# A second xT buffer, one q/k buffer, w2 ahead of batch 2's loads, and attention paced per batch, in a fused attention and feed-forward kernel

## The chip, the cores and the metric

The kernel runs on one core of a Trainium2 chip. The metric is device time in microseconds (us), the median of several executions. A program on one core has no second die to compare with, so a run counts as slow only when it is over 1.5% above the fastest of its kernel. TensorE is the matmul engine (PE in the profile), VectorE is DVE, ScalarE is ACT, GpSimd is POOL, and SyncE is SP.

## The reference

Relu-squared attention over 8 batches, 12 heads, 448 tokens and 64 columns a head, followed by a feed-forward block with layer norm and a residual:

```python
scores = (q @ k.transpose(0, 1, 3, 2)) / np.sqrt(64)
attn   = np.maximum(scores, 0.0) ** 2 / 448
x      = (attn @ v)                       # heads joined: (8, 448, 768)
xn     = (x - mu) / np.sqrt(var + 1e-06) * g_ln
out    = x + np.maximum(xn @ w_ch1, 0.0) @ w_ch2     # 768 -> 3072 -> 768
```

Batches are counted from 0 here, so "batch 2" is the third. Inputs and output are fp32, the kernel computes in bf16, and its loads cast while they move.

## The kernel before

The feed-forward work is done in four units of two batches. Attention of later batches is threaded between its matmuls: each piece of feed-forward work has a cost, and a target says how many attention steps must be out by then. So the order of the pieces matters: in the trace below TensorE stands for 3.57 us at one product with v while feed-forward matmuls come next in its program. Names in the code and the profile: QK are the matmuls of the scores (sc), AV those with v, at the squared scores, xT the attention output x with its columns on the partitions, x_t the same x with tokens on the partitions, xc the centred x that goes into the feed-forward, h1 the output of the first feed-forward pass. These parts matter (the rest is cut):

```python
io_pool = ctx.enter_context(tc.tile_pool(name="qkv", bufs=2))   # q, k, v
xT_pool = ctx.enter_context(tc.tile_pool(name="xT", bufs=1))
...
def load_batch(b, pieces):            # all on GpSimd's queue, with the cast
    ...                               # from batch 2 on q and k head by head: 24 loads of 56 KB
def att_T(i, ...):                    # head pair i: q and k transposed
    if b >= PE_T:                     # from batch 2 on by DMA, on SyncE's queue
        for t, sb in enumerate((q_sb, k_sb)):
            nc.sync.dma_start_transpose(qkT_t[:, t, :]..., sb[:, 2*pr:2*pr+2, :]...)
def att_AV(i, ...):
    ...                               # 8 matmuls, then VectorE:
    nc.vector.tensor_scalar(xT_of(b, pr), ps, c2, None, op0=Alu.mult)
def ffn_x(u, ki):                     # tokens back to partitions, for statistics and residual
    nc.sync.dma_start_transpose(x_tok[u][:, :, ki*P:(ki+1)*P], xT[u][:, ki, :])
...
load_batch(2, ALL)                    # batch 2, then w2
for c in range(W2C):
    load_w2(c)
...
def pull():                           # emits an attention step; then
    while nload < B and ai >= steps_of(nload - 2):
        load_batch(nload, ALL)        # batch 3 as soon as batch 1's attention is emitted
```

xT holds the attention output of the two batches of a unit. `ffn_x` reads it, and attention of the next unit overwrites it.

Of the kernel before, what the change touches and what calls it, by code (L numbers as in the profile page):

```python
# [11 lines left out]
def kernel(  # L12
# [10 lines left out]
    nc = tc.nc  # L23
    P = 128
    bf16 = mybir.dt.bfloat16
# [4 lines left out]
    B, H, S, D = q.shape  # L30
# [5 lines left out]
    NJ = 4  # L36
    SP = S // NJ
    NPAIR = H // 2
    K1 = d_model // P
    K2 = d_ff // P  # L40
    U = 2
# [6 lines left out]

    const_pool = ctx.enter_context(tc.tile_pool(name="const", bufs=1))
    w_pool = ctx.enter_context(tc.tile_pool(name="w_pool", bufs=1))  # L50
    io_pool = ctx.enter_context(tc.tile_pool(name="qkv", bufs=2))
    t_pool = ctx.enter_context(tc.tile_pool(name="qkT", bufs=3))
    attn_pool = ctx.enter_context(tc.tile_pool(name="attn", bufs=7))
    xT_pool = ctx.enter_context(tc.tile_pool(name="xT", bufs=1))
    xs_pool = ctx.enter_context(tc.tile_pool(name="xs", bufs=1))
    xc_pool = ctx.enter_context(tc.tile_pool(name="xc", bufs=2))
    x_pool = ctx.enter_context(tc.tile_pool(name="x", bufs=1))
# [16 lines left out]
    h1 = h_pool.tile([P, K2, UT], bf16)  # L74
# [2 lines left out]


    qkv = {}

    PE_T = 2

    def load_batch(b, pieces):

        if b not in qkv:
            q_sb = io_pool.tile([SP, H, NJ * D], bf16, tag="q_sb")
            k_sb = io_pool.tile([SP, H, NJ * D], bf16, tag="k_sb")
            v_sb = io_pool.tile([SP, H, NJ * D], bf16, tag="v_sb")
            qkv[b] = (q_sb, k_sb, v_sb)
        q_sb, k_sb, v_sb = qkv[b]  # L90
        pairs = {"q": (q_sb, q), "k": (k_sb, k), "v": (v_sb, v)}
        for name, h0, hs in pieces:
            sb, src = pairs[name]
            if b >= PE_T and name != "v":

                by_pair = sb.rearrange("p (a x) (j d) -> p a (x j d)", x=2, j=NJ)
                by_pair = by_pair.rearrange("p a (j x d) -> p a j x d", x=2, j=NJ)
                for a in range(h0 // 2, (h0 + hs) // 2):
                    for x in range(2):
                        nc.gpsimd.dma_start(  # L100
                            by_pair[:, a, :, x, :],
                            src[b, 2 * a + x].rearrange("(p j) d -> p j d", j=NJ))
                continue
            nc.gpsimd.dma_start(  # L104
                sb[:, h0:h0 + hs, :],
                src[b, h0:h0 + hs].rearrange("h (p j) d -> p h (j d)", j=NJ),
            )

    g_sb = const_pool.tile([P, K1], fp32)

# [2 lines left out]
    def load_early():  # L113
# [10 lines left out]
            cast(dst, st)  # L124
        with nc.allow_non_contiguous_dma(reason="768 gains, once"):
            nc.sync.dma_start(g_sb, moe_g_ln.rearrange("(ko kp) -> kp ko", kp=P))

    ALL = [(n, 0, H) for n in "qkv"]

    CH = 512  # L130
    NCH = d_ff // CH
# [2 lines left out]
    def load_w1(c):  # L134
        nc.gpsimd.dma_start(w1[:, :, c * CH:(c + 1) * CH], w1_view[:, :, c * CH:(c + 1) * CH])
# [4 lines left out]
    def load_w2(c):  # L140
        ks = K2 // W2C
        nc.gpsimd.dma_start(w2[:, c * ks:(c + 1) * ks, :], w2_view[:, c * ks:(c + 1) * ks, :])

    def prep_w1(c, eng, k0, k1):
        for ki in range(k0, k1):
            w = w1[:, ki, c * CH:(c + 1) * CH]
            eng.tensor_scalar(w, w, g_sb[:, ki:ki + 1], None, op0=Alu.mult)  # L147


    xT = {}  # L150
# [5 lines left out]
    def att_T(i, half=None, evac=True):  # L156
        b, pr = divmod(i, NPAIR)
        q_sb, k_sb, _ = qkv[b]
        if b >= PE_T:
            if half == 0:  # L160
                return
            qkT_t = t_pool.tile([P, 2, S], bf16, tag="qkT")
            qkT[i] = qkT_t
            for t, sb in enumerate((q_sb, k_sb)):
                nc.sync.dma_start_transpose(
                    qkT_t[:, t, :].rearrange("p (j s) -> p j s", j=NJ),
                    sb[:, 2 * pr:2 * pr + 2, :].rearrange("p x e -> p (x e)"))
            return
        if half != 1:
            tp_ps = ps_m.tile([P, 2, S], bf16, tag="m")  # L170
            tp[0] = tp_ps
        ps = tp[0]
        for t, sb in enumerate((q_sb, k_sb)):
            if half is not None and t != half:
                continue
            for j in range(NJ):
                for hh in range(2):
                    nc.tensor.transpose(
                        ps[hh * D:(hh + 1) * D, t, j * SP:(j + 1) * SP],
                        sb[:, 2 * pr + hh, j * D:(j + 1) * D],  # L180
                        identity[:SP, :SP])
        if half == 0 or not evac:
            return
        att_T_out(i)

    def att_T_out(i):
        qkT_t = t_pool.tile([P, 2, S], bf16, tag="qkT")
        qkT[i] = qkT_t
        nc.vector.tensor_copy(qkT[i], tp[0])
# [61 lines left out]
    def ffn_x(u, ki):  # L251
        if ki == 0:
            x_t = x_pool.tile([P, MU, d_model], bf16, tag="x")
            x_tok[u] = x_t
        nc.sync.dma_start_transpose(x_tok[u][:, :, ki * P:(ki + 1) * P], xT[u][:, ki, :])  # L255
# [62 lines left out]
    att = []  # L318
# [6 lines left out]
    def step_b(i):  # L325
        att_QK(i, 2)
        att_QK(i, 3)
        if i > 0:
            att_AV(i - 1)
        if i + 2 < PE_T * NPAIR:  # L330
            att_T(i + 2)
        if PE_T * NPAIR <= i + 3 < NP_ALL:
            att_T(i + 3)

    def step_fine(i):
        att_QK(i, 0)
# [45 lines left out]
    def steps_of(b):  # L382
        return done_at[b]

    NU = B // U
    segs = []
    CPN = K2 // NCH
    for u in range(NU):
        for bb in range(U):
            items = []  # L390
            for ni in range(K2):
                if bb == 0 and u == 0 and ni % CPN == 0 and ni // CPN + 1 < NCH:
                    c = ni // CPN + 1
                    items.append((0.0, lambda c=c: prep_w1(c, nc.vector, K1 // 2 if c < 3 else 0, K1)))
                if bb == 1 and ni == 0:
                    for ki in range(K1):
                        items.append((0.0, lambda u=u, ki=ki: ffn_x(u, ki)))
                if bb == 1 and ni >= K2 - MU:
                    items.append((0.0, lambda u=u, m=ni - (K2 - MU): ffn_stats(u, m)))
                items.append((1.12, lambda u=u, bb=bb, ni=ni: ffn_1(u, bb, ni)))  # L400
            segs.append((u * U + bb, items))
        items = []
        for m in range(MU):
            for j in range(2):
                for part in range(4):
                    items.append((0.96, lambda u=u, m=m, j=j, p=part: ffn_2(u, m, j, p, 4)))
                    if m + j + part == 0:
                        items.append((0.0, lambda u=u: ffn_stats(u, MU)))
        segs.append((u * U + U - 1, items))
# [2 lines left out]
    ENGINES = [E.PE, E.Pool, E.DVE, E.Activation, E.SP]  # L412

    ai = 0
    nload = 3

    def pull():
        nonlocal ai, nload
        att[ai]()
        ai += 1  # L420
        while nload < B and ai >= steps_of(nload - 2):
            load_batch(nload, ALL)
            nload += 1

    with tc.manual_schedule(engines=set(ENGINES)):
        load_batch(0, [("v", 0, 4), ("q", 4, 4), ("k", 4, 4), ("v", 4, 4),
                       ("q", 8, 4), ("k", 8, 4), ("v", 8, 4)])
        load_early()
        load_w1(0)
        load_batch(1, ALL[:2])  # L430
        load_w1(1)
        load_batch(1, ALL[2:])
        for c in range(2, NCH):
            load_w1(c)
        for c in range(3):
            prep_w1(c, nc.gpsimd, 0, K1 // 2 if c else K1)
        warm_up(20)
        att_T(0)
        warm_up(5)
        while ai < steps_of(0):  # L440
            pull()
        load_batch(2, ALL)
        for c in range(W2C):
            load_w2(c)

        bounds = {}
        total = 0.0
        cum = []
        for need, items in segs:
            total += sum(c for c, _ in items)  # L450
            cum.append(total)
        t1 = cum[0]
        t_end = cum[-1] - sum(c for c, _ in segs[-1][1]) - sum(c for c, _ in segs[-2][1])
        n0, n1, n2 = steps_of(0), steps_of(1), len(att)

        def target(t):
            if t <= t1:
                return n0 + (n1 - n0) * t / (t1 - 3.0)
            return n1 + (n2 - n1) * (t - t1) / (t_end - 9.0 - t1)

        t = 0.0
        for need, items in segs:
            while ai < steps_of(need):
                pull()
            for cost, fn in items:
                fn()
                t += cost
                while ai < len(att) and ai + 1 <= target(t):
                    pull()
        assert ai == len(att) and nload == B  # L470


# [28 lines left out]
```

## Time and profile before

| | before |
|---|---|
| median of 3 runs | 587.07 us (586.45 to 588.53) |
| profiled span | 586.3 us |
| TensorE busy | 569.4 us |

First the busy table of the page (busy us, share of the span, instructions):

```profile
PE 569.4 (97%) x3542; PEld 289.1 (49%) x3542; DVE 262.5 (45%) x505; ACT 266.7 (45%) x392; POOL 142.5 (24%) x188
```

TensorE is the bottleneck, and a busy TensorE may still be at half clock. So look for its gaps and for stretches of low clock. The table by stretches of the kernel before (TensorE's idle time is the length less PE busy; then the other engines, the mean granted clock, the DMA share and GB/s):

```profile
72.40:90.00 17.60, 17.44 (x99) 8.23 (x98) 9.39 (x17) 11.72 (x19) 2.11 (x3) 1.00 1.18 192
90.00:112.00 22.00, 22.00 (x129) 10.19 (x127) 1.25 (x2) 14.54 (x24) 8.55 (x13) 1.00 1.53 166
112.00:126.00 14.00, 10.43 (x48) 4.38 (x45) 11.11 (x26) 4.48 (x6) 11.04 (x16) 0.76 1.93 170
126.00:136.00 10.00, 7.82 (x41) 3.78 (x40) 7.40 (x17) 3.63 (x5) 10.00 (x16) 0.83 1.43 85
...
220.00:240.00 20.00, 19.27 (x109) 8.71 (x108) 7.58 (x14) 11.58 (x20) 0.94 (x1) 1.00 0.83 121
```

The loss lies between 112 and 136 us: 5.75 us idle, and a clock of 0.76 and 0.83. The waits of that stretch name the first cause (who waited for what: us in total, times, longest; three of the lines):

```profile
DVE xT_t L230 <- DMA x_t<-xT_t: 20.2, 1, 20.2
...
PE av_ps L223 <- DVE at L200: 3.6, 1, 3.6
...
PE sc L197 <- ACT at L199: 2.2, 2, 1.8
```

VectorE may not write batch 2's output into xT until `ffn_x` has read it. It stands 20.2 us, then has a backlog, and TensorE waits for its squares. TensorE's timeline there (start, us, instructions; idle time and releaser in brackets):

```profile
108.22 3.58 PE L278 MATMUL ps<-xc_t,w_109 128*128 128x448 bf16 x18
111.73 0.58 PE L197 MATMUL sc<-qkT_t 64*112 64x448 bf16 x4
115.89 2.19 PE L223 MATMUL av_ps<-at,v_sb 112*64 112x448 bf16 x8 [3.57 <-DVE at L200]
118.01 4.37 PE L278 MATMUL ps<-xc_t,w_109 128*128 128x448 bf16 x12
```

Eighteen feed-forward matmuls take 3.58 us at full clock. After the gap twelve take 4.37 us, about half speed. The trace's clock records give half clock for 6.83 us from 115.1 and 3.41 us from 132.2.

What kept the transposes so long? SyncE's and GpSimd's queues (three lines of the first, four of the second):

```profile
79.40 5.22 SPq L165 DMA_TRANSPOSE qkT_t<-k_sb  x1
84.67 23.55 SPq L255 DMA_TRANSPOSE x_t<-xT_t  x6
108.31 1.21 SPq L165 DMA_TRANSPOSE qkT_t<-q_sb  x1
```

### The profile page before, as it was taken

The page shows a single profiled execution, that of the slowest core. Times are in us where ns is not written, and L with a number is a line of the kernel's source. Part 1 is how long each engine was busy: PE and PEld are TensorE (multiplying, and loading weights), DVE is VectorE, ACT ScalarE, POOL GpSimd, SP SyncE. Part 2 cuts the span into 40 slices and gives each one's busy share as a digit, 9 for nine tenths or more (in the row PEclk, how much of TensorE's full clock was granted, in tenths as well). Part 3 has the DMA queues.
Part 4 walks back from the last instruction along what each step waited for, and adds up shares of the span by engine and source line. Part 5 has one row for each costly group of instructions (what it writes and reads, how often), then busy time and mean ns, then how long its engine had stood idle before and what let it go on. Part 6 is the DMA issues. An engine that isn't in the chain of part 4 may idle for free.

```text
span 586.3 us, 8930 instructions
## 1 busy us (share of the span) xinstructions
PE 569.4 (97%) x3542; PEld 289.1 (49%) x3542; DVE 262.5 (45%) x505; ACT 266.7 (45%) x392; POOL 142.5 (24%) x188
## 2 busy tenths in 40 slices
PE   8989999789999999999999999999999999999996
PEld 5444444345555444445555444445555545556663
DVE  5967850194454433275453434257454435201111
ACT  6937866533233575663323465764313364440000
POOL 7788611683004600083002800000000000000000
PEclk9989999988999999999999999999999999999999
DMA  9999999999536909298264915610223141000111
GB/s 179 202 205 123 138 190 183 149 141 87 86 85 95 126 17 123 51 86 84 59 118 60 152 29 72 101 33 17 70 50 79 30 87 32 0 2 28 55 54 55
DMA packets 153242, 51.79 MB, mean 88 GB/s; under 512 B 125808, under 2 KB 149616, under 8 KB 153200
## 3 DMA queue, kind: packets, MB, share of 16 engines
q0 software_dynamic: 90144, 25.50, 44.6%
q1 hardware_dynamic: 62576, 25.25, 22.6%
q8 instruction: 28, 0.46, 0.3%
q10 hardware_dynamic: 480, 0.46, 0.3%
q14 instruction: 14, 0.11, 0.1%
HBM read 51.91 MB, written 11.01 MB: 107 GB/s over the span
## 4 chain that ended last, share of the span: by engine, by line
PE 76%; DMA 12%; DVE 4%; SPq 4%; POOL 3%; issue 1%; ACT 0%; DVEq 0%; POOLq 0%
PE o_ps L294 37%; PE ps L278 28%; DMA w_109<-in_moe_w_ch_dram 7%; PE sc L197 6%; PE av_ps L223 5%; DMA w_110<-in_moe_w_ch_dram 4%; SPq L255 3%; DMA x_t<-xT_t 2%; POOL k_sb L100 1%; DVE xc_t L245 1%; DVE at L200 1%; DVE stats L272 1%; POOL v_sb L104 1%; DVE stats L271 1%; POOL q_sb L100 1%
## 5 line engine op out<-in xcount | busy, mean ns | idle before, releaser
L278 PE MATMUL ps<-xc_t,w_109 128*128 128x448 bf16 x1152 | 232.2, 356 | 2.5 <-DVE xc_t L245 2.5
L294 PE MATMUL o_ps<-w_110,h_111 128*128 128x384 bf16 x1344 | 226.9, 327 | 0.0
L199 ACT ACTIVATE at<-sc 112x896 bf16<-112x896 f32 x192 | 165.1, 916 | 135.8 <-PE sc L197 132.2
L200 DVE TENSOR_TENSOR at<-at 112x896 bf16<-112x896 bf16 x192 | 118.9, 629 | 172.1 <-ACT at L199 172.1
L294 PEld LDWEIGHTS <-h_111 128*128 128x128 bf16 x1344 | 129.0, 98 | 96.4 <-issue 14.4
L278 PEld LDWEIGHTS <-w_109 128*128 128x128 bf16 x1152 | 109.4, 98 | 117.8 <-issue 21.5
L280 ACT ACTIVATE h_111<-ps 128x448 bf16<-128x448 f32 x192 | 104.6, 545 | 112.9 <-PE ps L278 112.8
L100 POOL DMA_DIRECT2D q_sb<-in_q_dram x72 | 50.2, 704 | 116.2 <-DMA qkT_t<-q_sb 53.1
L297 DVE SCALAR_TENSOR_TENSOR o_t<-o_ps,rstd_t,x_t 128x384 f32<-128x384 f32 x56 | 34.5, 616 | 76.9 <-PE o_ps L294 76.9
L197 PE MATMUL sc<-qkT_t 64*112 64x448 bf16 x384 | 59.7, 376 | 3.0 <-ACT at L199 2.7
L223 PE MATMUL av_ps<-at,v_sb 112*64 112x448 bf16 x384 | 48.7, 366 | 4.3 <-DVE at L200 3.6
L100 POOL DMA_DIRECT2D k_sb<-in_k_dram x72 | 50.0, 701 | 3.8 <-DMA q_sb<-in_q_dram 2.7
L230 DVE TENSOR_SCALAR xT_t<-av_ps 128x448 bf16<-128x448 f32 x48 | 29.7, 618 | 24.0 <-DMA x_t<-xT_t 20.2
L197 PEld LDWEIGHTS <-qkT_t 64*112 64x112 bf16 x384 | 18.6, 125 | 39.3 <-issue 37.2
L245 DVE TENSOR_TENSOR xc_t<-xT_t,mean_ps 128x448 bf16<-128x448 bf16 x48 | 26.2, 616 | 12.6 <-PE mean_ps L241 12.6
L223 PEld LDWEIGHTS <-v_sb 112*64 112x64 bf16 x384 | 17.8, 109 | 28.4 <-issue 22.1
L104 POOL DMA_DIRECT2D v_sb<-in_v_dram x10 | 8.9, 890 | 89.0 <-PE av_ps L223 88.3
L147 POOL TENSOR_SCALAR w_109<-w_109,g_sb 128x512 bf16<-128x512 bf16 x12 | 20.0, 1682 | 1.8 <-DVE w_109 L147 1.7
L272 DVE BATCH_NORM_STATS2 stats<-x_t 128x6 f32<-128x384 bf16 x28 | 15.2, 543 | 0.0
L271 DVE BATCH_NORM_STATS2 stats<-x_t 128x6 f32<-128x384 bf16 x28 | 14.6, 522 | 0.0
L315 PE MATMUL w_ps<-w_110,ones 128*128 128x256 bf16 x70 | 12.0, 315 | 1.2 <-DVE w_110 L76 1.2
L267 DVE RECIPROCAL rstd_t<-rstd_t 128x7 f32<-128x7 f32 x4 | 0.8, 200 | 26.7 <-ACT rstd_t L266 26.7
(32 smaller groups left out, 84.9 us busy)
## 6 DMA issues: line engine op xcount, KB each, us to landing
v_sb<-in_v_dram POOLq DMA_DIRECT2D x7, 672.0 KB, 10.1
w_109<-in_moe_w_ch_dram POOLq DMA_DIRECT2D x6, 768.0 KB, 25.6
w_110<-in_moe_w_ch_dram POOLq DMA_DIRECT2D x4, 1152.0 KB, 25.6
q_sb<-in_q_dram POOLq DMA_DIRECT2D x72, 56.0 KB, 3.9
k_sb<-in_k_dram POOLq DMA_DIRECT2D x72, 56.0 KB, 4.0
out_dram<-o_t SPq DMA_DIRECT2D x8, 336.0 KB, 3.0
out_dram<-o_t SPq DMA_DIRECT2D x8, 288.0 KB, 2.7
out_dram<-o_t SPq DMA_DIRECT2D x8, 240.0 KB, 2.8
```

The costliest lines, as they stand in the source:

```text
L100: nc.gpsimd.dma_start(by_pair[:, a, :, x, :], src[b, 2 * a + x].rearrange("(p j) d -> p j d", j=NJ))
L197: nc.tensor.matmul(sc[:SP, hh, :S], qkT[i][r, 1, t * SP:(t + 1) * SP], qkT[i][r, 0, :], start=True, stop=True)
L199: nc.scalar.activation(at, sc[:SP, :, :S], Act.Relu)
L200: nc.vector.tensor_mul(at, at, at)
L223: nc.tensor.matmul(ps[hh * D:(hh + 1) * D, :], v_sb[:, 2 * pr + hh, t * D:(t + 1) * D], attn[i, t][:, hh, :], start=(t == 0), stop=(t == N ...
L230: nc.vector.tensor_scalar(xT_of(b, pr), ps, c2, None, op0=Alu.mult)
L245: nc.vector.tensor_sub(xc_t[:, ki, :], xT_of(b, ki), mean_ps)
L272: nc.vector.bn_stats(stats[:, 1], x_tok[u][:, m, hd:])
L278: nc.tensor.matmul(ps, w1[:, ki, ni * P:(ni + 1) * P], xc[u * U + bb][:, ki, :], start=(ki == 0), stop=(ki == K1 - 1))
L280: nc.scalar.activation(h1[:, ni, bb * S:(bb + 1) * S], ps, Act.Relu)
L294: nc.tensor.matmul(o_sb[1], h1[:, ki, m * P:(m + 1) * P], w2[:, ki, j * hd:(j + 1) * hd], start=(ki == 0), stop=(ki == K2 - 1))
L297: nc.vector.scalar_tensor_tensor(o_sb[0][:, j * hd:(j + 1) * hd], o_sb[1], rstd[u][:, m:m + 1], x_tok[u][:, m, j * hd:(j + 1) * hd], op0=A ...
```

## The change

The intent: two xT buffers, so that the 20 us wait goes. SBUF has no room for that beside two buffers of q and k, so q and k get one, and batch 1's q and k live in the half of h1 that the first feed-forward pass doesn't use. Batch 2's loads move behind w2, batch b+1's loads follow the last transpose of batch b, x_t's six transposes are spread over six steps, and attention is paced to end 3 or 5 cost units ahead of each need. The order within a batch changes too: before it was all of q, all of k, then v; now q and k come pair by pair, with v behind the second pair. The core of the diff (cut; `load_pair` loads one pair's q and k, a head at a time as before):

```diff
-    io_pool = ctx.enter_context(tc.tile_pool(name="qkv", bufs=2))
+    io_pool = ctx.enter_context(tc.tile_pool(name="qkv", bufs=1))
+    v_pool = ctx.enter_context(tc.tile_pool(name="v", bufs=2))
-    xT_pool = ctx.enter_context(tc.tile_pool(name="xT", bufs=1))
+    xT_pool = ctx.enter_context(tc.tile_pool(name="xT", bufs=2))
+    def alloc_batch(b):
+        v_sb = v_pool.tile([SP, H, NJ * D], bf16, tag="v_sb")
+        if b == 1:
+            half = h1[:SP, :, S:S + NJ * D]
+            qkv[b] = (half[:, :H, :], half[:, H:2 * H, :], v_sb)
+            return
...
+    def load_paired(b):
+        alloc_batch(b)
+        for a in range(NPAIR):
+            load_pair(b, a)
+            if a == 1:
+                load_heads(b, [("v", 0, H)])
...                                    # step_b(i)
+        b, r = divmod(i + 4, NPAIR)
+        if r == 0 and PE_T < b < B:
+            load_paired(b)
...
-                if bb == 1 and ni == 0:
-                    for ki in range(K1):
-                        items.append((0.0, lambda u=u, ki=ki: ffn_x(u, ki)))
+                if bb == 1 and ni < K1:
+                    items.append((0.0, lambda u=u, ki=ni: ffn_x(u, ki)))
...
-        load_batch(2, ALL)
         for c in range(W2C):
             load_w2(c)
+        load_paired(2)
...                                    # one line per stage, not one for all
+                pace.append((t - 5.0 if need > 1 else t - 3.0, steps_of(need)))
```

More of the change, by code (lines that the diff above doesn't have):

```diff
@@ L81, with load_heads @@
     PE_T = 2
-    def load_batch(b, pieces):
-        if b not in qkv:
-            q_sb = io_pool.tile([SP, H, NJ * D], bf16, tag="q_sb")
-            k_sb = io_pool.tile([SP, H, NJ * D], bf16, tag="k_sb")
-            v_sb = io_pool.tile([SP, H, NJ * D], bf16, tag="v_sb")
-            qkv[b] = (q_sb, k_sb, v_sb)
+    PE_T = 2
+    def alloc_batch(b):
[4 more added lines that the diff above has]
+            return
+        q_sb = io_pool.tile([SP, H, NJ * D], bf16, tag="q_sb")
+        k_sb = io_pool.tile([SP, H, NJ * D], bf16, tag="k_sb")
+        qkv[b] = (q_sb, k_sb, v_sb)
+    def load_heads(b, pieces):
         q_sb, k_sb, v_sb = qkv[b]
@@ L93, in load_batch @@
             sb, src = pairs[name]
-            if b >= PE_T and name != "v":
-                by_pair = sb.rearrange("p (a x) (j d) -> p a (x j d)", x=2, j=NJ)
-                by_pair = by_pair.rearrange("p a (j x d) -> p a j x d", x=2, j=NJ)
-                for a in range(h0 // 2, (h0 + hs) // 2):
-                    for x in range(2):
-                        nc.gpsimd.dma_start(
-                            by_pair[:, a, :, x, :],
-                            src[b, 2 * a + x].rearrange("(p j) d -> p j d", j=NJ))
-                continue
             nc.gpsimd.dma_start(
@@ L107, in load_batch, with load_pair @@
             )
+    def load_pair(b, a):
+        for sb, src in zip(qkv[b], (q, k)):
+            by_pair = sb.rearrange("p (a x) e -> p a (x e)", x=2)
+            by_pair = by_pair.rearrange("p a (j x d) -> p a j x d", x=2, j=NJ)
+            for x in range(2):
+                nc.gpsimd.dma_start(
+                    by_pair[:, a, :, x, :],
+                    src[b, 2 * a + x].rearrange("(p j) d -> p j d", j=NJ))
+    def load_paired(b):
[4 more added lines that the diff above has]
+                load_heads(b, [("v", 0, H)])
     g_sb = const_pool.tile([P, K1], fp32)
@@ L126, in load_early @@
             nc.sync.dma_start(g_sb, moe_g_ln.rearrange("(ko kp) -> kp ko", kp=P))
-    ALL = [(n, 0, H) for n in "qkv"]
     CH = 512
@@ L414 @@
     ai = 0
-    nload = 3
     def pull():
-        nonlocal ai, nload
+        nonlocal ai
         att[ai]()
         ai += 1
-        while nload < B and ai >= steps_of(nload - 2):
-            load_batch(nload, ALL)
-            nload += 1
     with tc.manual_schedule(engines=set(ENGINES)):
-        load_batch(0, [("v", 0, 4), ("q", 4, 4), ("k", 4, 4), ("v", 4, 4),
+        alloc_batch(0)
+        load_heads(0, [("v", 0, 4), ("q", 4, 4), ("k", 4, 4), ("v", 4, 4),
                        ("q", 8, 4), ("k", 8, 4), ("v", 8, 4)])
@@ L429 @@
         load_w1(0)
-        load_batch(1, ALL[:2])
+        alloc_batch(1)
+        load_heads(1, [("q", 0, H), ("k", 0, H)])
         load_w1(1)
-        load_batch(1, ALL[2:])
+        load_heads(1, [("v", 0, H)])
         for c in range(2, NCH):
@@ L441 @@
             pull()
-        load_batch(2, ALL)
         for c in range(W2C):
             load_w2(c)
-        bounds = {}
-        total = 0.0
-        cum = []
+        load_paired(2)
+        pace = [(0.0, steps_of(0))]
+        t = 0.0
         for need, items in segs:
-            total += sum(c for c, _ in items)
-            cum.append(total)
-        t1 = cum[0]
-        t_end = cum[-1] - sum(c for c, _ in segs[-1][1]) - sum(c for c, _ in segs[-2][1])
-        n0, n1, n2 = steps_of(0), steps_of(1), len(att)
+            if need % U == 1 and items is segs[need // U * (U + 1) + 1][1]:
+                pace.append((t - 5.0 if need > 1 else t - 3.0, steps_of(need)))
+            t += sum(c for c, _ in items)
         def target(t):
-            if t <= t1:
-                return n0 + (n1 - n0) * t / (t1 - 3.0)
-            return n1 + (n2 - n1) * (t - t1) / (t_end - 9.0 - t1)
+            for (ta, na), (tb, nb) in zip(pace, pace[1:]):
+                if t <= tb:
+                    return na + (nb - na) * (t - ta) / (tb - ta)
+            return len(att)
         t = 0.0
@@ L469 @@
                     pull()
-        assert ai == len(att) and nload == B
+        assert ai == len(att)
 _INS = ['q', 'k', 'v', 'moe_g_ln', 'moe_w_ch1', 'moe_w_ch2']
```

## The prediction

> **What bounds it now.** TensorE: busy 569.4 of 586.3 us (busy table), 76% of the chain of waits. Only its gaps and the half-clock stretches after them can be won. In the timeline and the clock records the largest loss after the first 40 us lies at 112 to 136 us. VectorE waits 20.2 us, once, at the evacuation into xT, for the DMA transposes x_t<-xT (table of waits): with one xT buffer batch 2 can't write until xT of batches 0 and 1 has been read out, at 114.3 us. TensorE then idles 3.57 us (from 112.3) and, with VectorE catching up on squares and statistics, 1.77 + 0.41 us at 129 to 131 us. The clock is at half for 6.8 us after the first and 3.4 us after the second; half speed loses half of that: 5.75 + 5.1 = 10.9 us. The Trainium skill ("TensorE: Matmul & The Clock Gate", Part 1) describes such a gate with a window of about 3.4 us; the records agree.
>
> The transposes are slow because from 72 to 98 us the queues alternate w2's 1536-byte packets (113 a us) with their 256-byte packets (110 a us): round robin per packet, as in the Trainium skill ("DMA: Bandwidth & Descriptors", Queues, rings and completion order).
>
> **What the change does.**
> 1. xT doubled: the 20.2 us wait goes, and with it both stalls: -10.9 us, all on the path.
> 2. Pace with 4 to 5 us of margin: TensorE's waits for xc at 226 us (0.7) and 362 us (0.15) go: -0.9.
> 3. w2 ahead of batch 2's q/k: this costs. GpSimd reaches these loads at 42.3 us in both, and the queue is full of w1 until 49.2. Now batch 2's first pair is transposed from 59.9 us and its first QK runs at 73.4. After the change it stands behind 4.7 MB of w2. w1 moved at 208 GB/s undisturbed, so I estimate 22 to 23 us: w2 done at about 71, pair one landed at 73 to 74, its two DMA transposes (1.2 us issue each, 2.6 to landing, more beside other packets) at 77 to 78.5. Batch 1's pace is unchanged, so TensorE reaches that QK at 73.4, stalls about 4.3 us, and runs one or two windows at half clock: 1.7 to 3.4 more. Together +6 to +8 us.
> 4. One q/k buffer: loads of batch b+1 wait for the last transpose of batch b, then take 24 issues of 0.7 us, first needed over 25 us later: hidden. Batch 1's q/k in h1: loaded at 8.5 us, read before that half is written: free.
>
> TensorE's own work is the same.
>
> **Sum.** 587.1 - 10.9 - 0.9 + 6.5 = about 581.8 us; 8 in 10 between 576 and 587. Without the new stall it would be 575.3, just at 2%. Chances: faster by over 2% 0.15, within 2% 0.83, slower 0.02.
>
> **What would show it.** (1) No wait of the xT evacuation for x_t; no TensorE gap and full clock from 100 to 136 us. (2) No gap before the first FFN matmuls of batches 2 and 4. (3) w2 landing at 70 to 73 us, TensorE idle 3 to 6 us before batch 2's first QK near 73 us, half clock after it. (4) Later transposes wait for loads, TensorE doesn't. Start to 73 us unchanged.
>
> **What would make it wrong.** w2 at the 113 packets a us seen beside transposes: the stall is 8 us and the gain nearly gone. w2 faster, or QK later: no stall, 575. Statistics colliding with attention on VectorE although xT is free: part of the 10.9 stays. Hidden dependencies of batch 1's q/k inside h1.

## More of the kernel before

```profile
62.25 3.35 POOL L142 DMA_DIRECT2D w_110<-in_moe_w_ch_dram  x4
...
99.31 0.70 POOL L100 DMA_DIRECT2D q_sb<-in_q_dram  x1 [5.92 <-DMA w_110<-in_moe_w_ch_dram]
...
105.18 1.39 POOL L100 DMA_DIRECT2D k_sb<-in_k_dram  x2 [0.22 <-issue]
...
116.92 0.94 POOL L104 DMA_DIRECT2D v_sb<-in_v_dram  x1
```

The transposes share the DMA engines first with w2 (until about 98 us) and then, from 99 to 117 us, with loads of batch 3.

## The result, and the profile after

| | before | after |
|---|---|---|
| median | 587.2 us (4 runs) | 586.25 us (4 runs, 585.57 to 586.55) |
| ratio | | 0.998 (95%: 0.9959 to 1.000): same |
| profiled span | 586.3 us | 583.8 us |
| TensorE busy | 569.4 us | 563.6 us |

A ratio is the mean time of one kernel's fast runs over that of the other's fast runs of the same rounds, so it is not quite the ratio of the medians quoted. The span above belongs to the fastest of the four runs after. The busy table of the kernel after:

```profile
PE 563.6 (97%) x3542; PEld 287.3 (49%) x3542; DVE 263.6 (45%) x505; ACT 266.7 (46%) x392; POOL 143.3 (25%) x188
```

The same stretches as before:

```profile
72.40:90.00 17.60, 8.67 (x41) 3.41 (x41) 4.62 (x9) 5.69 (x8) 12.15 (x18) 0.71 1.85 136
90.00:112.00 22.00, 21.85 (x126) 10.16 (x125) 9.02 (x17) 14.38 (x23) 0.00 (x0) 1.00 0.58 92
112.00:126.00 14.00, 14.00 (x81) 6.48 (x80) 9.47 (x23) 9.33 (x16) 11.35 (x16) 1.00 0.97 81
126.00:136.00 10.00, 10.00 (x67) 5.26 (x65) 6.00 (x14) 5.48 (x9) 5.60 (x9) 1.00 1.87 133
...
220.00:240.00 20.00, 20.00 (x113) 9.59 (x112) 7.09 (x13) 12.52 (x21) 0.00 (x0) 1.00 0.50 78
```

Everything that the change aimed at happened. From 112 to 136 us TensorE is never idle and the clock is full, and the gap at 220 to 240 us is gone. But 72 to 90 us, nearly full before, now has 8.9 us idle and a clock of 0.71. TensorE's waits (the two largest) and timeline of the kernel after:

```profile
PE sc L209 <- DMA qkT_t<-k_sb: 8.9, 1, 8.9
PE ps L290 <- DVE xc_t L257: 1.8, 7, 0.7
```
```profile
71.16 1.31 PE L290 MATMUL ps<-xc_t,w_112 128*128 128x448 bf16 x6
81.40 1.00 PE L209 MATMUL sc<-qkT_t 64*112 64x448 bf16 x4 [8.93 <-DMA qkT_t<-k_sb]
82.33 2.42 PE L290 MATMUL ps<-xc_t,w_112 128*128 128x448 bf16 x6
```

The first scores (QK) of batch 2 wait 8.93 us for the transposed k of its first head pair. The clock records show half clock for 10.24 us from 75.97; 4.8 us of that (81.40 to 86.22) is work, so 2.4 us are lost. GpSimd's and SyncE's queues in the kernel after show why the k is late:

```profile
42.53 3.35 POOL L154 DMA_DIRECT2D w_113<-in_moe_w_ch_dram  x4
45.84 1.42 POOL L112 DMA_DIRECT2D q_sb<-in_q_dram  x2
...
54.77 0.70 POOL L112 DMA_DIRECT2D q_sb<-in_q_dram  x1 [4.88 <-DMA w_113<-in_moe_w_ch_dram]
...
71.81 0.70 POOL L112 DMA_DIRECT2D k_sb<-in_k_dram  x1 [5.10 <-DMA w_113<-in_moe_w_ch_dram]
72.50 0.95 POOL L101 DMA_DIRECT2D v_sb<-in_v_dram  x1
```
```profile
72.27 1.29 SPq L177 DMA_TRANSPOSE qkT_t<-q_sb  x1
73.67 1.20 SPq L177 DMA_TRANSPOSE qkT_t<-k_sb  x1
```

w2's last piece has landed at 71.8 us. The two transposes of the first pair start at 72.27 and 73.67, so its loads had landed by then; so far the prediction was within 1 us. But k is usable only at 81.4 us, 7.7 us after its transpose was issued. The packet records of the trace, with the transposes' packets counted off in order (448 each), show it. "First" and "last" are us from issue to first and last packet, and the right side is what else moved meanwhile, by bytes per packet:

```
kernel after
72.27 q transpose: first 1.37 last 2.18 | 128 B x1141, 512 B x3
73.67 k transpose: first 3.86 last 6.50 | 128 B x439, 512 B x1334
```

512-byte packets are the v load. From 74.5 to 77.5 us it moved about 760 packets and the k transpose none. In later batches of this trace too, the transposes with over 800 of v's packets beside them took 6.0 to 9.6 us. Whether v is the cause is tested in e3.

### The profile page after: what moved, and what is told of

It reads as the page before. It is cut to its first block, busy times and chain, and to the rows that moved or that the text cites. A ratio compares the mean times of both kernels' runs of the same rounds, so it can differ in the third digit from the quotient of the medians.

```text
span 583.8 us, 8969 instructions
## 1 busy us (share of the span) xinstructions
PE 563.6 (97%) x3542; PEld 287.3 (49%) x3542; DVE 263.6 (45%) x505; ACT 266.7 (46%) x392; POOL 143.3 (25%) x188
## 4 chain that ended last, share of the span: by engine, by line
PE 90%; DVE 5%; DMA 2%; ACT 1%; issue 0%; SPq 0%; ACTq 0%
PE o_ps L306 38%; PE ps L290 37%; PE sc L209 7%; PE av_ps L235 6%; DVE at L212 2%; ACT at L211 1%; DMA qkT_t<-k_sb 1%; DVE xc_t L257 1%; DMA h_114<-in_q_dram 1%; DVE qkT_t L201 1%; DVE xT_t L242 0%; DVE xs_t L246 0%; PE tp_ps L190 0%; PE mean_ps L253 0%; PE mean_ps L252 0%
## 5 line engine op out<-in xcount | busy, mean ns | idle before, releaser
L212 DVE TENSOR_TENSOR at<-at 112x896 bf16<-112x896 bf16 x192 | 120.2, 632 | 184.2 <-ACT at L211 184.2
L235 PE MATMUL av_ps<-at,v_sb 112*64 112x448 bf16 x384 | 47.3, 361 | 1.0 <-DVE at L212 0.6
L246 DVE TENSOR_TENSOR xs_t<-xs_t,xT_t 128x448 bf16<-128x448 bf16 x24 | 10.0, 416 | 0.8
```

The lines of the kernel that those rows point to most:

```text
L212: nc.vector.tensor_mul(at, at, at)
L235: nc.tensor.matmul(ps[hh * D:(hh + 1) * D, :], v_sb[:, 2 * pr + hh, t * D:(t + 1) * D], attn[i, t][:, hh, :], start=(t == 0), stop=(t == N ...
```

## Experiments

Eleven runs, all correct. Runs of one call share a chip and the runs of the kernel before; the calls are e1 to e4, e5 to e8, and e9 to e11. All kernels but e9 are edits of the kernel after.

| run | median us | before | ratio (95%) | longest TensorE wait after 40 us |
|---|---|---|---|---|
| e1 batch 2 ahead of w2 | 574.51 | 588.47 | 0.9756 (0.9734 to 0.9779) | 0.16 |
| e2 first pair ahead | 577.13 | 588.47 | 0.980 (0.9779 to 0.982) | 2.63 |
| e3 v last | 582.33 | 588.47 | 0.9887 (0.987 to 0.9904) | 6.42 |
| e4 three of four pieces ahead | 579.55 | 588.47 | 0.9838 (0.9812 to 0.9863) | 3.10 |
| e5 e1 with one xT | 575.68 | 587.34 | 0.9802 (0.9785 to 0.982) | 0.67 |
| e6 e1 with the old pace | 576.16 | 587.34 | 0.9805 (0.9787 to 0.9822) | 0.18 (four times) |
| e7 after with one xT | 586.59 | 587.34 | 0.9983 (0.9965 to 1.0001) | 9.13 |
| e8 e2 with v last | 582.9 | 587.34 | 0.9922 (0.9905 to 0.9938) | 6.92 |
| e9 before, batch 3 late | 579.74 | 587.95 | 0.9858 (0.9831 to 0.9886) | 2.02 |
| e10 e1 again | 575.05 | 587.95 | 0.9788 (0.9764 to 0.9813) | 0.16 |
| e11 e5 again | 575.87 | 587.95 | 0.9796 (0.9774 to 0.9818) | 0.53 |

### e1: batch 2 ahead of w2

Two theories of the missing gain. A: it was real and was turned into a new wait. B: it would be lost later anyway, because the transposes into x_t still share the queues with w2.

```diff
+        load_paired(2)
         for c in range(W2C):
             load_w2(c)
-        load_paired(2)
```

> The kernel after, with batch 2's q, k and v put back ahead of w2 and nothing else changed. Theory A (the gain was real and was turned into a new stall by putting w2 ahead): the wait of TensorE for the transpose of batch 2's first k (8.9 us) and the half clock after it (4.8 us of work at half, 2.4 us lost) go, the wait for xT stays away; 586.2 - 11.3 = about 575 us, ratio to before 0.975 to 0.983, TensorE without a gap of over 1 us from 60 to 140 us. Rival B (the time comes back later: w2's packets now share the queues with the transposes into x_t again, so the statistics on VectorE wait for x_t and hold attention up): 580 to 586 us, with TensorE gaps of 2 to 8 us between 105 and 135 us.

It took 574.51 us, ratio 0.9756. TensorE's waits in e1, complete:

```profile
PE ps L290 <- DVE xc_t L257: 1.8, 7, 0.7
PE w_ps L327 <- DVE w L77: 1.2, 1, 1.2
PE sc L209 <- DVE qkT_t L201: 0.9, 2, 0.7
PE tp_ps L190 <- DVE xT_t L242: 0.8, 1, 0.8
PE sc L209 <- ACT at L211: 0.5, 3, 0.2
PE av_ps L235 <- DVE xT_t L242: 0.2, 1, 0.2
```

The 8.9 us line is gone and nothing took its place. All waits over 0.2 us lie in the first 40 us. Theory A holds and B falls. This order is also the version that beats both kernels.

### e4: three of w2's four pieces ahead

```diff
-        for c in range(W2C):
+        for c in range(W2C - 1):
             load_w2(c)
         load_paired(2)
+        load_w2(W2C - 1)
```

> The kernel after, with three of the four pieces of w2 ahead of batch 2 and the fourth behind. Theory A with w2 at the 5.7 us a piece that the profile after shows: batch 2's first pair is usable 5.7 us earlier, the stall falls from 8.9 to about 3.2 us, one window of half clock instead of three; about 579 us. If the stall doesn't come from the bytes of w2 ahead of the pair, it stays near 9 us and 586.

The wait of e4:

```profile
76.06 0.59 PE L209 MATMUL sc<-qkT_t 64*112 64x448 bf16 x4 [3.10 <-DMA qkT_t<-k_sb]
```

The stall fell from 8.93 to 3.10 us, which is one piece of w2 (5.7 us), and one window of half clock (3.41 us) followed it. With four pieces ahead the stall is 8.93 us, with three 3.10, and with none (e1) there is none: the bytes ahead of the pair set most of it. The v load, next, sets the rest.

### e3: v behind all six pairs

Why 8.9 us and not the predicted 4.3? Theory C blames the v load beside the k transpose. Rival D says that any backlog does it.

```diff
-            if a == 1:
+            if a == (NPAIR - 1 if b == PE_T else 1):
                 load_heads(b, [("v", 0, H)])
```

> The kernel after, with batch 2's v loaded behind all six head pairs and not behind the second. It tells apart why the stall was 8.9 us and not the 4.3 predicted. Theory C (the v load, 512-byte packets, keeps the transpose of the first k from the queues: its last packet left 6.5 us after its issue against 2.2 for q): with v out of the way the k transpose takes 3 to 4 us, the stall is 5 to 6.5 us, and the time is 582 to 584 us. Rival D (the transposes are slow behind any backlog of loads, or w2 is simply late): the stall stays at 8 to 9 us and the time at 586.

The wait of e3 and its first two transposes (the second fence from packet records, as before):

```profile
78.15 0.99 PE L209 MATMUL sc<-qkT_t 64*112 64x448 bf16 x4 [6.42 <-DMA qkT_t<-k_sb]
```
```
e3
72.22 q transpose: first 1.28 last 2.84 | 128 B x1750
73.63 k transpose: first 1.41 last 2.82 | 128 B x1422
```

With 128-byte loads beside it, the k transpose needs 2.82 us instead of 6.50. The stall is 6.42 us, the time 582.33 us: theory C. A backlog of 128-byte loads stands beside the transposes here too, so rival D falls. k is now usable at 78.15 us, within the predicted 77 to 78.5. The remaining 6.4 us goes when w2 isn't ahead (e1).

### e2 and e8: only the first pair ahead of w2

In e2 batch 2's first pair goes ahead of w2 and the rest stays behind:

```diff
+        alloc_batch(2)
+        load_pair(2, 0)
         for c in range(W2C):
             load_w2(c)
         load_paired(2)                # without the allocation and pair 0
```

> The kernel after, with only the four loads of batch 2's first head pair ahead of w2, all the rest behind it. Theory A: only the first pair is late, the second is needed some 10 us later; the stall goes and the time is within 1 us of e1 (about 575 us). If the stall comes from the whole backlog of batch 2 (each pair late), TensorE stalls at the QK of the second pair instead, by 2 us or more, and the time lies 3 us or more above e1.

Theory A's "only the first pair is late" was a miss: e2 is 2.6 us slower than e1. The stall moved to the second pair. Its k transpose was issued at 76.28 us, and its last packet came 5.93 us later, again with v's packets beside it. e8 puts v last in e2 as well:

> e2 (only the first head pair ahead of w2) with batch 2's v behind all pairs, a second test of theory C. In e2 TensorE still waited 2.6 us, for the k of the second pair, whose transpose took 5.9 us beside the v load. Theory C: without v beside it that transpose takes 3 to 4 us, the 2.6 us stall goes to under 0.5 us, and the time falls from 577.1 to about 574.5, that of e1. If v has no part in it, the stall and the 577 stay.

e8 took 582.9 us and not 574.5. The lines of e2 and of e8, one each:

```profile
83.67 0.59 PE L210 MATMUL sc<-qkT_t 64*112 64x448 bf16 x4 [2.63 <-DMA qkT_t<-k_sb]
```
```profile
94.52 1.70 PE L236 MATMUL av_ps<-at,v_sb 112*64 112x448 bf16 x8 [6.92 <-DMA v_sb<-in_v_dram]
```

The mechanism was right: the second pair's k transpose took 2.81 us to its last packet and the 2.63 us wait is gone. But the expectation forgot who needs v. v was now issued at 83.59 us, landed beside the transposes of x_t at 94.5, and AV of batch 2, ready at 87.6, waited 6.92 us for it. In e8, moving v only moved the wait to another consumer. Of the orders tried, only that of e1, with all of batch 2 ahead of w2, leaves no such wait.

### e5, e10, e11: one xT buffer

The prediction credited the second xT buffer with 10.9 us. e5 takes it away from e1:

```diff
-    xT_pool = ctx.enter_context(tc.tile_pool(name="xT", bufs=2))
+    xT_pool = ctx.enter_context(tc.tile_pool(name="xT", bufs=1))
```

> e1 (the kernel after with batch 2 ahead of w2) with xT back to one buffer. It measures the doubled xT by itself. Theory A (as predicted: without the second xT TensorE stalls): a wait of VectorE for x_t of 10 us or more, TensorE stalls of 3 us or more near 110 us, 580 us or more. Rival E (the wait was long only because batch 3's loads and w2 crowded the transposes; with one q/k buffer batch 3's loads come after 112 us and x_t is read out by 107 us, while TensorE first needs what VectorE holds up at about 112 us): VectorE waits 5 to 15 us, TensorE not at all or under 1 us, and the time is within 1.5 us of e1 (about 574.5).

> e1 once more, on the same chip and in the same rounds as e11 and e9: again about 0.976 to 0.979 of the kernel before (574.5 us). It is the reference for e11.

> e5 once more (e1 with one xT buffer), beside e10. Theory E: within 0.25% of e10 (0 to 1.5 us slower; the profile of e5 showed one TensorE wait of 0.7 us more). If the second xT buffer matters, 2 us or more slower than e10.

e5 took 575.68 us. Side by side on one chip, e10 took 575.05 and e11 575.87 us: 0.9788 and 0.9796 of the kernel before, with overlapping intervals. VectorE's wait and the only new TensorE wait of e5 over 0.15 us:

```profile
DVE xT_t L242 <- DMA x_t<-xT_t: 16.0, 1, 16.0
```
```profile
126.16 4.06 PE L306 MATMUL o_ps<-w,h 128*128 128x384 bf16 x24 [0.67 <-DVE o_t L309]
```

VectorE does wait 16.0 us, until 106.2 us, and it costs TensorE 0.67 us (0.53 in e11). The 20.2 us wait before, until 114.7 us, cost it 10.5. Attention has seven buffers of scores between the two engines, and TensorE first needs what VectorE holds up at about 109 us in e5 and 112 us in the kernel before. VectorE is back in time in the one and not in the other; a wait shorter than that slack is nearly free.

### e7: the kernel after with one xT buffer

The edit is that of e5, on the kernel after.

> The kernel after with xT back to one buffer (w2 stays ahead). The x_t transposes end at about 104 us there and batch 2's first evacuation into xT comes at 101 us, so VectorE should wait about 3 us and TensorE not: 586 us, as after, the stall of 8.9 us near 72 us unchanged. If the second xT buffer is what removed the stalls at 112 to 131 us, they come back: 590 us or more.

It took 586.59 us, ratio 0.9983, against 0.998 for the kernel after: the stall (9.13 us) is the same, VectorE waited 3.6 us until 106.4 us, and no TensorE wait came back at 112 us. The second buffer does nothing measurable for the kernel as changed either.

### e9: the kernel before, with batch 3's loads held back

If not the second buffer, what cured the stalls at 112 to 131 us? Theory E: with one q/k buffer, batch 3's loads can't start until batch 2's last transpose, and so they no longer crowd the transposes of x_t. In the kernel after they start at 114.0 us, before at 65 us, the bulk moving from 99 us on. e9 does this alone, in the kernel before:

```diff
-        while nload < B and ai >= steps_of(nload - 2):
+        while nload < B and ai >= steps_of(nload - 2) + (2 if nload == 3 else 0):
+            if nload == 3:
+                nc.gpsimd.tensor_copy(mark, x_tok[0][:, MU - 1, d_model - 1:])
             load_batch(nload, ALL)
```

> The kernel before with one thing alone: batch 3's loads wait (by a one-element copy on GpSimd that reads x_t) until x_t of batches 0 and 1 has landed; xT single, two q/k buffers, old pace, old order. Theory E (what made the x_t transposes so late before were batch 3's loads in the same queues, and not needing one xT buffer is what the change really bought by its single q/k buffer): x_t lands at 104 to 108 us and not 114, VectorE waits 10 to 14 us and not 20, TensorE stalls under 1 us near 112 to 131, about 575 to 577.5 us, near e6. If the second xT buffer, the pace or the spread x_t issues are needed too, the stalls stay at 3 us or more and the time is 581 or more.

```profile
106.86 0.19 POOL L424 COPY mark<-x_t 128x1 bf16<-128x1 bf16 x1 [41.48 <-DMA x_t<-xT_t]
```
```profile
123.14 0.54 PE L198 MATMUL sc<-qkT_t 64*112 64x448 bf16 x2 [2.02 <-ACT at L200]
```

x_t landed at 106.9 us instead of 114.3, VectorE's wait fell from 20.2 to 13.6 us, and the stall of 3.57 us at 112 us is gone. The time is 579.74 us, 8.2 us better than the kernel before, but not the 575 to 577.5 expected. A second, smaller stall (2.02 and 0.27 us, 6.83 us of half clock) stays at 121 to 124 us, when VectorE works off its backlog and the statistics. So theory E explains the larger part. e6 (old pace, two xT) and e5 (new pace, spread x_t, one xT) are each free of that second stall. They differ from e9 in several things, and share the spread x_t transposes and the pair-by-pair loads. Which part of the change removes it was not separated, and the second buffer isn't shown to.

### e6: the old pace

e1 with the old pacing lines put back.

> e1 with the pace of the kernel before. It measures the new pace by itself. As predicted: TensorE waits for xc again before the first FFN matmuls of batch 2 (0.7 us near 215 us) and perhaps of batch 4 (0.15 us), 0.5 to 1.5 us slower than e1. Rival: no measurable difference and no new gap.

576.16 us. The profile shows four waits of 0.18 us for xc at 217 to 219 us, 0.7 us together, as predicted. As e6 and e1 ran in different calls (0.9805 against 0.9756 and 0.9788), the times confirm no more than a small loss.

## Why the prediction was right and wrong

The time, 586.25 us, lies inside the stated range, and the class (within 2%) had 0.83. But the forecast was a gain of 5.4 us, and 1 us came. Point by point:

- **"TensorE's gaps at 112 to 136 us go: -10.9 us."** They went, in full. By the later reading, in which 0.76 us of the first half-clock stretch are idle anyway, they were worth 5.75 + (6.07 + 3.41)/2 = 10.5 us.
- **"xT doubled: the 20.2 us wait goes, and with it both stalls, all on the path."** The size was right, but the second buffer was not what earned it. e10 and e11 differ by 0.8 us, e7 shows nothing, and e9 gets most of it with one buffer. (Whether the second buffer alone would have done it, with batch 3's loads still early, no run shows: it doesn't fit.) The reading of the trace had stopped at w2's packets (until 98 us) and had not asked what crowded the transposes from 99 to 114 us: batch 3's loads. The Trainium skill ("DMA: Bandwidth & Descriptors", Issuing engines are not separate DMA queues) says that transfers issued from different engines run on the same 16 DMA engines and interleave; the trace of before agrees, with x_t's last transposes taking 7.3 to 7.9 us to their last packet there and 2.5 to 3.5 us in e10.
- **"Pace: -0.9."** The gaps at 226 and 362 us are gone; e6 brings back 0.7 us. Right.
- **"w2 ahead of batch 2's q/k: +6 to +8."** This is the step that failed, by size. The place, the cause, w2's end (71 predicted, 71.8 seen) and the landing of the pair (73 to 74, about 72 to 73.7) were right. The term "its two DMA transposes at 77 to 78.5" was not: k was usable at 81.4, because v's load held its transpose to 6.5 us (e3: 2.8 without it, and k usable at 78.15). TensorE also reached this QK 0.9 us earlier (72.5; e3, e4 and e7, with the same TensorE program up to that QK, reached it between 71.7 and 73.8). So the stall was 8.9 us and not 4.3, and with 2.4 us of half clock the term is 11.3, not 6.5. Put into the sum: -10.9 - 0.9 + 11.3 = -0.5 us, against -0.95 measured. The prediction's own warning named the wrong reason for a stall of that length (w2 at 113 packets a us); w2 moved faster, at 133 to 137 packets a us between 48 and 68 us.
- **"One q/k buffer: hidden; batch 1 in h1: free."** Right: no TensorE wait in e1 belongs to either.
- **"Without the new stall 575.3."** e1 took 574.51 and e10 575.05 us.

So the gain was on the critical path. It was made, and paid back 40 us earlier, by one line of load order.

## What to carry to other kernels

When a change moves loads, list for each consumer when it reaches its data and everything that stands ahead of it in the queue: a weight needed at 126 us must not go ahead of a small load needed at 72. A long wait of an engine off the bottleneck is not a cost as such; ask when the bottleneck would next need it, and which other traffic made it long, before paying memory for a second buffer. Price a small transfer at its duration beside what will run next to it, not alone.

## What the Trainium skill lacked or had wrong

- "DMA: Bandwidth & Descriptors" (Queues, rings and completion order) describes round robin between the queues, and w2 beside transposes agrees: from 72 to 98 us of the kernel before, 107 and 109 packets a us in the mean (the prediction had 113 and 110). It doesn't prepare for a transpose that starts beside the v load: its first packet left 3.86 us after issue, its last after 6.50 us, against 1.41 and 2.82 beside 128-byte loads (e3). A fair alternation from the start would not leave it without one packet from 74.5 to 77.5 us. The runs don't show the reason.
- No page has the duration of a DMA transpose beside other loads. In the kernel after, one of q or k took 1.9 us from issue to last packet in most cases with the other queue empty, and 2.2 to 4.9 us beside 128-byte loads. The rules of "DMA: Bandwidth & Descriptors" (Rules for kernel authors) say only that a transpose next to ordinary DMAs needs nothing, which is about correctness.
- "TensorE: Matmul & The Clock Gate" (Part 1) gives half clock after at least one idle window of about 3.4 us. Less idle time sufficed here. In these traces the clock records change only at the ends of steps of 3.41 us. From 28 to 555 us, over all thirteen profiles, the 14 steps after which the clock fell held 1.28 to 3.41 us of TensorE idle time (2.64 in e2, 2.02 in e9), no other step at full clock held more than 1.26, and full clock came back after the first step without idle time. So the cost depends on where a wait falls in the steps: 6.42 us of waiting (e3) cost 6.83 us of half clock, 6.92 us (e8) cost 10.24.
